# Two experts' scores in one visit of TensorE, new prices in a kernel's own list scheduler, and an order searched again

## The chip, the cores and the metric

The kernel runs on one core of a Trainium2 chip. Its engines work side by side: TensorE (PE in the profile, and PEld for its weight loads), VectorE (DVE), ScalarE (ACT), GpSimd (POOL) and SyncE (SP), which issues nearly all DMA transfers. The metric is the device time of one execution in microseconds; lower is better.

## The reference, cut to what matters

Four sequences of 576 tokens and width 512 pass through three stages. The second is the one whose code changes.

```python
# 1. windowed attention: 8 heads of 64; heads 0-3 see 32 keys back, heads 4-7 every 4th of 128 back
x = attn_out.transpose(0, 2, 1, 3).reshape(B, S, H * D)
# 2. mixture of E = 4 attention experts, the best K = 2 per token
for e in range(E):
    q, k, v = x @ wq[e], x @ wk[e], x @ wv[e]            # 64 wide
    scores = np.where(causal, -1e9, scale * (q @ k.transpose(0, 2, 1)))
    scores = scores - scores.max(-1, keepdims=True)
    a = np.exp(scores); a /= a.sum(-1, keepdims=True) + 1e-09
    ye = a @ v @ wo[e]                                   # added where e is among the best K, times its weight
# 3. layer norm, then x + relu(xn @ w_ch1) @ w_ch2, 512 -> 2048 -> 512
```

## The kernel before

All matrix products of fp32 data are made from pairs: a value rounded for TensorE ("h") and the rest ("l"), so a product is three matmuls (h·h, h·l, l·h). In the scores the two rests are packed: `KH` holds an expert's rounded keys on both halves of the partitions, `SQ` the rounded queries and their rests, `KL` the rests of the keys, so that two matmuls (`SQ`·`KH`, line 934, and `SQ`·`KL`, line 935) give a score tile. A third (line 937) adds the causal mask of the diagonal block: bf16, the identity as weights, `mdiag` as the moving tensor, 64 or 128 columns wide.

The kernel isn't ordered by hand. Each piece of work is a generator, a *chain*, that yields the steps it wants to do with an engine and a price in ns: `op("PE", ns, deps)`. `run_chains` holds a clock for each engine and for PSUM's eight banks (`places["bank"]`). It takes, again and again, the step that could start earliest by these clocks, ties broken by the rank of the chain, and writes its instructions then. What it writes down is the final order on each engine; on the chip the engines only wait for one another's results. So the prices have no effect on the chip except through the order, and through `either`, which lets the list choose between engines for a step (a copy out of PSUM by ACT or DVE, a scaling by DVE, POOL or ACT). `MODE` is what the list adds when TensorE goes from full 128-row matmuls (`None`) to matmuls on 64-column tiles (`"columns"`) or 64 x 64 tiles (`"quarters"`) and back. `SHIFT` and `LEANING` hold one number each for every chain: the first moves its rank, the second (ns) its bias against the first engine of an `either`. Both lists were found by search.

The chains that matter here: `scores`, `window` and `mix` are stage 1 (lines 629, 648 to 667, 679, 714 to 733). `value_tile` (line 756) and `project` (line 854) make values, keys and queries of the experts. `attend(b, pr_, i)` runs for 4 sequences, 2 pairs of experts and 5 query tiles; tile i sees n = 64, 192, 320, 448 or 576 keys. In it, for each of the two experts `ee`, in turn: one bank of PSUM (two for n = 576), the two score matmuls and the mask matmul, `put("s", ...)` after the second, the row maximum by DVE (line 947), the exponential with its row sum by ACT (line 949), after which the bank is free. Then both experts' sums are turned into weights (lines 953 to 957), the probabilities scaled (line 961 for the first 64 keys, line 967 by ACT or 969 by DVE or POOL for the others), transposed on TensorE (lines 977, 995, 1011) and multiplied by the values (lines 1026 to 1034). `out_proj` (line 1090) applies `wo`. `decode` (lines 1189 to 1217) turns the 64-bit weights of stage 3 into pairs; `mlp_group` (lines 1367 and 1394) is stage 3. Nothing separates the stages but the data: matmuls of stage 3 start at about 257 us, while `attend` still runs.

Of the kernel before, what the change touches and what calls it, by code (L numbers as in the profile page):

```python
# [39 lines left out]
]  # L40
LEANING = [
# [16 lines left out]
def windowed_attention_moe_mlp(  # L58
# [20 lines left out]
    P = 128  # L79
# [109 lines left out]
    for x in range(3):  # L189
# [18 lines left out]
    shared = {"DVE": 0.0, "POOL": 0.0}  # L208
    facts, chains, mode = {}, [], [None]
    shifts, leaning = list(SHIFT), list(LEANING)  # L210
    MODE = {(None, "columns"): 165.0, (None, "quarters"): 75.0, ("columns", None): 120.0, ("quarters", None): 100.0,
            ("columns", "quarters"): 65.0, ("quarters", "columns"): 65.0}

    def op(engine, ns, deps=(), tile=None):
# [1273 lines left out]
```

## Time and profile before

| what | value |
|---|---|
| median of 3 runs | 689.91 us (687.67 to 690.09) |
| the profiled execution | 688.62 us, of which the span from the first to the last instruction is 686.9 us |
| TensorE busy, weight loads busy | 672.9 us (98%), 568.8 us (83%) |
| VectorE, ScalarE, GpSimd busy | 497.7 us, 313.6 us, 197.6 us |
| granted clock of TensorE | 1.00 of full speed |

Busy time is the union of an engine's instructions. Matmuls overlap in the records (each lasts longer than the distance to the next one's start), so the cost of a matmul is read from start to start.

### The profile page before, as it was taken

To read this page: it belongs to the slowest core of one execution; us is meant where nothing else is said; L and a number is where in the kernel's file an instruction comes from. 1 tells how busy PE (TensorE), PEld (TensorE's weight loads), DVE (VectorE), ACT (ScalarE), POOL (GpSimd) and SP (SyncE) were. 2 spreads that over 40 slices of the span, in tenths; PEclk is the share of its full clock that TensorE was granted. 3 is DMA by queue.
4 is the path that set the end of the run, shared out by engine and by line. 5 is a ranking of instruction groups with operands and counts; after the bars stand their busy time and mean duration, and the time that the engine had idled before them with its cause. 6 is when DMAs were issued, how large, how long until landed. Compare 5 with 4: busy or idle time off the path is not lost.

```text
span 686.9 us, 13791 instructions
## 1 busy us (share of the span) xinstructions
PE 672.9 (98%) x5215; PEld 568.8 (83%) x5215; DVE 497.7 (72%) x1077; ACT 313.6 (46%) x879; POOL 197.6 (29%) x261
## 2 busy tenths in 40 slices
PE   7999999999999999999999999999999999999998
PEld 5788798988989887888888888888888888888886
DVE  6768999889888998988887755845755845754344
ACT  4767876888787889743322311211222211310110
POOL 3742112103211555565343321410422320410000
PEclk9999999999999999999999999999999999999999
DMA  9873643270403325335111200110111200100123
GB/s 175 206 154 94 107 89 69 53 125 12 103 16 128 108 82 180 106 103 176 43 62 62 62 31 31 62 31 1 62 62 32 62 31 2 60 1 0 62 92 123
DMA packets 111362, 52.55 MB, mean 77 GB/s; under 512 B 81472, under 2 KB 104512, under 8 KB 111296
## 3 DMA queue, kind: packets, MB, share of 16 engines
q1 hardware_dynamic: 110128, 51.38, 28.8%
q8 instruction: 41, 0.67, 0.4%
q10 hardware_dynamic: 1168, 0.29, 0.2%
q14 instruction: 25, 0.20, 0.1%
HBM read 39.86 MB, written 9.44 MB: 72 GB/s over the span
## 4 chain that ended last, share of the span: by engine, by line
PE 91%; DVE 4%; SPq 2%; ACT 1%; DMA 1%; issue 1%; POOL 0%; DVEq 0%; POOLq 0%
PE psall L1367 29%; PE psall L1394 29%; PE psall L854 7%; PE psall L756 4%; PE psall L1090 3%; PE psall L1034 2%; PE psall L714 2%; PE psall L679 2%; PE psall L934 2%; PE psall L1011 2%; PE psall L935 2%; PE psall L629 1%; PE psall L1032 1%; PE psall L565 1%; SPq L361 1%; DVE sm L663 1%
## 5 line engine op out<-in xcount | busy, mean ns | idle before, releaser
L1367 PE MATMUL psall<-xn,wp 128*128 128x512 f32 (+1 forms) x960 | 218.6, 372 | 0.0
L1394 PE MATMUL psall<-wp,ht 128*128 128x512 f32 (+1 forms) x870 | 217.0, 393 | 0.0
L1367 PEld LDWEIGHTS psall<-xn,wp 128*128 128x128 f32 x960 | 168.2, 188 | 34.7 <-issue 0.3
L1394 PEld LDWEIGHTS psall<-wp,ht 128*128 128x128 f32 x870 | 161.1, 188 | 36.5 <-issue 0.3
L1372 ACT ACTIVATE ht<-psall 128x512 fp32r<-128x512 f32 (+1 forms) x80 | 44.4, 554 | 221.0 <-PE psall L1367 211.3
L1403 DVE SCALAR_TENSOR_TENSOR x2a<-psall,rstd,x2a 128x512 f32<-128x512 f32 x124 | 91.7, 747 | 50.2 <-PE psall L1394 49.3
L1374 DVE SCALAR_TENSOR_TENSOR ht<-psall,ht 128x512 fp32r<-128x512 f32 (+1 forms) x80 | 50.8, 635 | 63.8 <-ACT ht L1372 63.5
L1205 POOL TENSOR_TENSOR d_pw<-d_pw,d_t 128x512 f32<-128x512 f32 x32 | 41.6, 1301 | 187.4 <-DVE d_pw L1202 184.8
L1217 POOL TENSOR_TENSOR wp<-d_pw,wp 128x512 fp32r<-128x512 f32 x32 | 42.5, 1328 | 28.8 <-ACT wp L1215 28.7
L949 ACT ACTIVATE Pp<-psall,nm 128x64 f32<-128x64 f32 (+4 forms) x80 | 42.3, 530 | 7.4 <-DVE nm L947 6.5
L947 DVE TENSOR_REDUCE nm<-psall 128x1 f32<-128x192 f32 (+4 forms) x80 | 38.1, 483 | 5.9 <-PE psall L937 4.7
L1215 ACT CAST wp<-d_pw 128x512 fp32r<-128x512 f32 x32 | 19.8, 620 | 48.9 <-DVE d_pw L1208 28.2
L667 POOL TENSOR_TENSOR sc<-sc,rs 128x480 f32<-128x480 f32 (+1 forms) x26 | 25.3, 975 | 52.1 <-DVE rs L665 47.6
L317 ACT COPY pT<-psall 80x288 f32<-80x288 f32 (+6 forms) x67 | 31.3, 476 | 12.3 <-PE psall L679 5.1
L1403 DVE SCALAR_TENSOR_TENSOR x2b<-psall,rstd,x2b 128x512 f32<-128x512 f32 (+1 forms) x33 | 24.2, 734 | 17.1 <-PE psall L1394 16.9
L1189 ACT ACTIVATE d_sq<-ws 128x512 f32<-128x512 f32 x32 | 21.5, 672 | 24.2 <-DVE d_pw L1208 18.0
L934 PE MATMUL psall<-KH,SQ 128*128 128x288 f32 (+4 forms) x96 | 31.8, 337 | 0.3 <-DVE xl L733 0.3
L1208 DVE SCALAR_TENSOR_TENSOR d_pw<-d_sq,d_pw 128x512 f32<-128x512 f32 x32 | 22.3, 696 | 11.0 <-POOL d_pw L1205 10.9
L679 PE MATMUL psall<-ident,sc 112*80 112x112 f32 (+1 forms) x168 | 25.2, 268 | 4.1 <-POOL sc L667 3.0
L935 PE MATMUL psall<-klz,SQ 128*128 128x288 f32 (+4 forms) x96 | 28.5, 302 | 0.0
L659 ACT ACTIVATE sc<-psall,mx 128x96 f32<-128x96 f32 (+1 forms) x113 | 27.4, 350 | 2.2 <-DVE mx L648 1.4
L1329 POOL TENSOR_TENSOR xn<-xt,xn 128x256 fp32r<-128x256 f32 (+1 forms) x24 | 22.8, 962 | 18.4 <-ACT xn L1325 15.4
(183 smaller groups left out, 1250.5 us busy)
## 6 DMA issues: line engine op xcount, KB each, us to landing
ws<-in_moe_w_ch_dram SPq DMA_DIRECT2D x32, 512.0 KB, 3.5
xd<-xg SPq DMA_DIRECT2D x18, 256.0 KB, 2.3
out_dram<-x2a SPq DMA_DIRECT2D x12, 256.0 KB, 2.0
xn<-xd SPq DMA_DIRECT2D x80, 32.0 KB, 1.8
KH<-KH SPq DMA_DIRECT2D x32, 72.0 KB, 2.0
natall<-in_q_dram SPq DMA_DIRECT2D x32, 72.0 KB, 2.6
natall<-in_k_dram SPq DMA_DIRECT2D x32, 72.0 KB, 2.3
xn<-xd SPq DMA_DIRECT2D x32, 64.0 KB, 2.8
```

The source lines that it names most:

```text
L679: nc.tensor.transpose(pt[:kw, P * (tt - a):P * (tt - a) + pw], sc[:pw, tt], ident[:pw, :pw])
L854: nc.tensor.matmul(pp[:, :HS], ws[:, c, pr_ * P:(pr_ + 1) * P], xs[:, c, cs], start=n == 0, stop=n == 3 * KC - 1)
L934: nc.tensor.matmul(ps[:m, :z - a], SQ[ee][:, q0:q0 + m], KH[ee][:, a:z], start=True, stop=False)
L935: nc.tensor.matmul(ps[:m, :z - a], SQ[ee][:, q0:q0 + m], KL[ee][:, a:z], start=False, stop=not end)
L949: nc.scalar.activation(pv, sv, AF.Exp, bias=nm[:m, ee:ee + 1], accum_out=sm[:m, ee:ee + 1])
L1205: nc.gpsimd.tensor_tensor(pf, pf, t1.bitcast(F32), op=ALU.add)
L1217: nc.gpsimd.tensor_tensor(lo, pf, hi.bitcast(F32), op=ALU.subtract)
L1367: nc.tensor.matmul(ph[:, :n_tok], ws[:, c * P:(c + 1) * P], xs[c], start=n == 0, stop=n == 3 * KC - 1)
L1372: nc.scalar.activation(hh[:, :n_tok], ph[:, :n_tok], AF.Relu)
L1374: nc.vector.scalar_tensor_tensor(hl[:, :n_tok], ph[:, :n_tok], 0.0, hh[:, :n_tok].bitcast(F32), op0=ALU.max, op1=ALU.subtract)
L1394: nc.tensor.matmul(po[:, :w], a_[:, sl], w_[:, cols], start=n == 0, stop=n == 3 * len(fs) - 1)
L1403: nc.vector.scalar_tensor_tensor(x2(i)[:, cols], po[:, :w], rstd[:, i:i + 1], x2(i)[:, cols], op0=ALU.mult, op1=ALU.add)
```

## The change

Five things change, all in the Python that writes the program.

1. In `attend`, tiles 0 to 3 do both experts' score matmuls in one step of TensorE. For i = 0 and 1 (n = 64 and 192) both experts share one bank, side by side; one mask matmul covers both diagonal blocks, one `tensor_reduce` gives both maxima. For i = 2 and 3 each expert has its bank; both banks are taken at once, the two mask matmuls follow one another, the two maxima stay apart. The exponentials stay two. Tile 4 keeps the old loop.
2. Prices in the list are set to others.
3. `MODE` gets other values, and SP steps get a `PATIENCE` of 27 ns in the comparison of start times (for the other engines it is 0 and changes nothing).
4. All of `SHIFT` and `LEANING` is replaced.
5. With 2 to 4 the order on every engine can differ everywhere, and so can the engine that an `either` picks.

```diff
 SHIFT = [
-    -2.04, -2.6, 4.96, -2.44, -0.7, 1.59, -0.29, 0.51, -0.3, -0.56, -2.11, 0.34, 0.68, -0.83, -0.79, -0.92, 1.36,
+    0.65, 0.67, 4.75, -1.44, -0.49, 1.13, 1.85, 1.2, -0.25, -0.36, 1, -0.24, 1.06, -0.58, -0.65, 0.61, 1.3, 0.94,
...
 LEANING = [
-    522, 471, 0, 71, 0, 0, 0, -105, 76, 0, 319, 0, 0, 0, 0, 0, 0, 0, 108, -52, 81, 243, 487, 28, 428, 453, 0, 0,
+    -226, -75, 0, 0, 0, 0, -113, 298, 43, 0, 319, 434, 0, 0, 128, 355, 343, 21, -348, 479, -384, 132, 736, 0, 632,
...
-    MODE = {(None, "columns"): 165.0, (None, "quarters"): 75.0, ("columns", None): 120.0, ("quarters", None): 100.0,
-            ("columns", "quarters"): 65.0, ("quarters", "columns"): 65.0}
+    PATIENCE = {"PE": 0.0, "ACT": 0.0, "DVE": 0.0, "POOL": 0.0, "SP": 27.0}
+    MODE = {(None, "columns"): 85.0, (None, "quarters"): 125.0, ("columns", None): 105.0, ("quarters", None): 105.0,
+            ("columns", "quarters"): 150.0, ("quarters", "columns"): 165.0}
...
-                    score = (at + change + sum(lean) + (0.0 if x or len(engines) == 1 else c[3]), c[0])
+                    score = (max(at + change, free[engine] + PATIENCE[engine]) + sum(lean) + (0.0 if x or len(engines) == 1 else c[3]), c[0])
...
-        t, e = yield either(("DVE*", dve(kw * nb)), ("POOL*", 1.98 * kw * nb), deps=[t])
+        t, e = yield either(("DVE*", dve(kw * nb)), ("POOL*", 2.08 * kw * nb + 20.0), deps=[t])
...
-            th = (yield op("ACT", act(n) + 20.0 + 0.85 * wide, [t, tx])) + 0.3 * wide
+            th = (yield op("ACT", act(n) + 30.0 + 0.95 * wide, [t, tx])) + 0.3 * wide
...
-        for ee in range(2):
+        if i < 4:
+            nb = 1 if i < 2 else 2
+            tb = yield acq("bank", nb)
+            pbs = [bank("s2") for _ in range(nb)]
+            pb = pbs[0]
+            w = n - q0
+            svs = [pb[:m, n * ee:n * ee + n] if nb == 1 else pbs[ee][:m, :n] for ee in range(2)]
+            t = yield op("PE", 4 * max(0.4415 * n + 5.0, 112.0) + 30.0 + 0.85 * w, [tb, tq])
+            for ee in range(2):
+                nc.tensor.matmul(svs[ee], SQ[ee][:, q0:q0 + m], KH[ee][:, :n], start=nb > 1 or not ee, stop=False)
+                nc.tensor.matmul(svs[ee], SQ[ee][:, q0:q0 + m], KL[ee][:, :n], start=False, stop=False)
+            if nb == 1:
+                both = pb[:m, :2 * n].rearrange("p (e n) -> p e n", e=2)
+                nc.tensor.matmul(both[:, :, q0:n], ident_bf, mdiag[:, None, :w].to_broadcast([P, 2, w]), start=False, stop=True)
+            else:
+                for ee in range(2):
+                    nc.tensor.matmul(svs[ee][:, q0:n], ident_bf, mdiag[:, :w], start=False, stop=True)
+            put("s", b, pr_, i, at=0.0)
+            tm = [t, t]
+            if nb == 1:
+                tm = [(yield op("DVE", dve(2 * n) + 20.0, [t]))] * 2
+                nc.vector.tensor_reduce(nm[:m], both, axis=AX.X, op=ALU.max, negate=True)
+            for ee in range(2):
+                Ps.append(Pp[:, ee])
+                if nb > 1:
+                    tm[ee] = yield op("DVE", dve(n) + 20.0, [t])
+                    nc.vector.tensor_reduce(nm[:m, ee:ee + 1], svs[ee], axis=AX.X, op=ALU.max, negate=True)
+                t1 = yield op("ACT", act(n) + 190.0, [tm[ee], tp])
+                nc.scalar.activation(Pp[:m, ee, :n], svs[ee], AF.Exp, bias=nm[:m, ee:ee + 1], accum_out=sm[:m, ee:ee + 1])
+                if nb > 1:
+                    give_bank(pbs[ee], t1)
+                tsum.append(t1)
+            if nb == 1:
+                give_bank(pb, t1)
+        for ee in range(2 if i > 3 else 0):
...
-                t = yield op("PE", 2 * max(0.4415 * (z - a) + 5.0, 90.0) + (100.0 if end else 0.0), [tb, tq])
+                t = yield op("PE", 2 * max(0.4415 * (z - a) + 5.0, 90.0) + (130.0 if end else 0.0), [tb, tq])
...
-                tpp[ee], e = yield either(("DVE*", 200.0 + 0.52 * (n - 64)), ("POOL*", 400.0 + 3.5 * (n - 64)), ("ACT", 135.0 + act(n - 64, False)), deps=[t])
+                tpp[ee], e = yield either(("DVE*", 200.0 + 0.52 * (n - 64)), ("POOL*", 330.0 + 2.8 * (n - 64)), ("ACT", 135.0 + act(n - 64, False)), deps=[t])
...
-        t = yield op("PE", 218.0 * (i + 1) if i else 125.0, tts + [tb], "columns" if i else None)
+        t = yield op("PE", 218.0 * (i + 1) + 30.0 if i else 125.0, tts + [tb], "columns" if i else None)
...
-        t = yield op("DVE", 340.0, [t, ta])
+        t = yield op("DVE", 440.0, [t, ta])
         nc.vector.tensor_scalar(t1, nh, 3, 0x3FFFFFF8, op0=ALU.logical_shift_left, op1=ALU.bitwise_and)
-        t = yield op("DVE*", 600.0, [t])
+        t = yield op("DVE*", 650.0, [t])
```

The other lines of the diff are of the last kind: prices of small DVE steps in the gate (80 to 160 ns before, 130 to 190 after), of the rest of `decode` (340 and 600 ns, now 440 and 650), of one scaling in `attend` (113, now 130), of the DVE step of `mix` and of a transpose in the layer norm.

## Rows read from the trace of the kernel before

**Rows 1.** The page: busy time of each engine, share of the span, instructions.

```profile
PE 672.9 (98%) x5215; PEld 568.8 (83%) x5215; DVE 497.7 (72%) x1077; ACT 313.6 (46%) x879; POOL 197.6 (29%) x261
```

**Rows 2.** The page: the chain that ended last, by engine.

```profile
PE 91%; DVE 4%; SPq 2%; ACT 1%; DMA 1%; issue 1%; POOL 0%; DVEq 0%; POOLq 0%
```

**Rows 3.** Busy by stretch: stretch, length, PE, PEld, DVE, ACT, POOL, clock, DMA.

```profile
100.00:130.00 30.00, 29.25 (x352) 26.04 (x351) 28.59 (x74) 22.32 (x74) 8.38 (x19) 1.00 0.28 62
...
160.00:190.00 30.00, 30.00 (x428) 27.49 (x426) 26.82 (x74) 25.27 (x81) 8.34 (x15) 1.00 0.29 66
...
250.00:281.00 31.00, 30.93 (x224) 24.93 (x223) 27.48 (x78) 28.70 (x85) 19.06 (x17) 1.00 0.46 141
```

**Rows 4.** The same view, before and after 281 us.

```profile
0.00:281.00 281.00, 270.20 (x3335) 238.46 (x3336) 239.61 (x663) 220.69 (x703) 93.55 (x170) 1.00 0.47 106
281.00:687.00 406.00, 402.66 (x1881) 330.38 (x1879) 258.11 (x414) 92.87 (x177) 104.02 (x92) 1.00 0.18 56
```

**Rows 5.** TensorE's waits from 15 to 281 us: total, times, longest; eight rows.

```profile
PE psall L679 <- POOL sc L667: 2.6, 5, 0.9
...
PE psall L679 <- DVE sc L667: 0.2, 1, 0.2
```

**Rows 6.** TensorE in order of time, visits among projections: start, length, instruction.

```profile
63.62 0.20 PE L934 MATMUL psall<-KH,SQ 128*128 128x64 f32 x1
63.65 0.27 PE L935 MATMUL psall<-klz,SQ 128*128 128x64 f32 x1
63.77 0.20 PE L937 MATMUL psall<-mdiag,ident_bf 128*128 128x64 bf16 x1
63.81 0.38 PE L854 MATMUL psall<-xh,wkh 128*128 128x288 f32 x1
64.02 0.29 PE L854 MATMUL psall<-xl,wkh 128*128 128x288 f32 x1
64.16 0.30 PE L854 MATMUL psall<-xh,wkl 128*128 128x288 f32 x1
...
64.79 0.23 PE L937 MATMUL psall<-mdiag,ident_bf 128*128 128x128 bf16 x1
64.83 0.38 PE L854 MATMUL psall<-xh,wqh 128*128 128x288 f32 x1
65.05 0.30 PE L854 MATMUL psall<-xl,wqh 128*128 128x288 f32 x1
```

**Rows 7.** All engines in order of time, a visit between transposes.

```profile
139.52 0.39 PE L934 MATMUL psall<-KH,SQ 128*128 128x320 f32 x1
...
139.75 0.31 PE L935 MATMUL psall<-klz,SQ 128*128 128x320 f32 x1
...
139.90 0.23 PE L937 MATMUL psall<-mdiag,ident_bf 128*128 128x128 bf16 x1
139.96 0.44 PE L1026 MATMUL psall<-pTh,V 128*128 128x128 f32 x2
```

**Rows 8.** DVE by line and form: busy, mean ns, idle before.

```profile
L947 DVE TENSOR_REDUCE nm<-psall 128x1 f32<-128x192 f32 x16 | 5.6, 351 | 1.3 <-PE psall L937 1.1
...
L947 DVE TENSOR_REDUCE nm<-psall 128x1 f32<-128x64 f32 x16 | 3.5, 218 | 0.6 <-PE psall L937 0.3
```

**Rows 9.** TensorE by line and form, the projections.

```profile
L854 PE MATMUL psall<-xh,wkh 128*128 128x288 f32 x64 | 21.8, 340 | 0.0
L854 PE MATMUL psall<-xh,wqh 128*128 128x288 f32 x64 | 21.0, 328 | 0.0
L854 PE MATMUL psall<-xl,wqh 128*128 128x288 f32 x64 | 18.8, 294 | 0.0
```

**Rows 10.** POOL by line and form, scalings that have a price in the list.

```profile
L667 POOL TENSOR_TENSOR sc<-sc,rs 128x480 f32<-128x480 f32 x20 | 20.3, 1016 | 47.5 <-DVE rs L665 44.8 <-ACT SQ L865 1.7 <-ACT sm L953 0.5
...
L969 POOL TENSOR_SCALAR Pp<-Pp,rs 128x256 f32<-128x256 f32 x3 | 2.9, 976 | 0.0
```

**Rows 11.** The widest scaling of `attend` on DVE, by line and form.

```profile
L969 DVE TENSOR_SCALAR Pp<-Pp,rs 128x512 f32<-128x512 f32 x7 | 3.3, 478 | 0.0
```

**Rows 12.** The same scaling on ACT, by line and form.

```profile
L967 ACT ACTIVATE Pp<-Pp,rs 128x512 f32<-128x512 f32 x8 | 5.7, 728 | 0.5 <-DVE rs L957 0.4
```

More of the change, by code (lines that the diff above doesn't have):

```diff
@@ L729, in mix @@
             wide = float(n) if dil else 0.0
-            th = (yield op("ACT", act(n) + 20.0 + 0.85 * wide, [t, tx])) + 0.3 * wide
+            th = (yield op("ACT", act(n) + 30.0 + 0.95 * wide, [t, tx])) + 0.3 * wide
             nc.scalar.copy(xv[0], pov)
-            tl = yield op("DVE", dve(n) + 20.0 + 0.72 * wide, [th])
+            tl = yield op("DVE", dve(n) + 30.0 + 0.85 * wide, [th])
             nc.vector.tensor_tensor(xv[1], pov, xv[0].bitcast(F32), op=ALU.subtract)
@@ L802, in gate @@
         row = [P, NT, E]
-        steps = [("DVE", 160.0, lambda n: n.tensor_tensor(gt, gj, ge, op=ALU.is_gt)),
-                 ("DVE", 160.0, lambda n: n.tensor_tensor(eq, gj, ge, op=ALU.is_equal)),
+        steps = [("DVE", 190.0, lambda n: n.tensor_tensor(gt, gj, ge, op=ALU.is_gt)),
+                 ("DVE", 190.0, lambda n: n.tensor_tensor(eq, gj, ge, op=ALU.is_equal)),
                  ("POOL", 340.0, lambda n: n.tensor_tensor(eq, eq, tri[:, None].to_broadcast(gb), op=ALU.mult)),
                  ("POOL", 340.0, lambda n: n.tensor_tensor(gt, gt, eq, op=ALU.add)),
-                 ("DVE", 160.0, lambda n: n.tensor_reduce(gw, gt, axis=AX.X, op=ALU.add)),
-                 ("DVE", 100.0, lambda n: n.tensor_reduce(gs, Gb, axis=AX.X, op=ALU.max)),
-                 ("DVE", 80.0, lambda n: n.tensor_scalar(gw, gw, 1.5, None, op0=ALU.is_lt)),
+                 ("DVE", 190.0, lambda n: n.tensor_reduce(gw, gt, axis=AX.X, op=ALU.add)),
+                 ("DVE", 150.0, lambda n: n.tensor_reduce(gs, Gb, axis=AX.X, op=ALU.max)),
+                 ("DVE", 130.0, lambda n: n.tensor_scalar(gw, gw, 1.5, None, op0=ALU.is_lt)),
                  ("POOL", 220.0, lambda n: n.tensor_tensor(ex, Gb, gs[:, :, None].to_broadcast(row), op=ALU.subtract)),
@@ L812, in gate @@
                  ("POOL", 220.0, lambda n: n.tensor_tensor(gw, gw, ex, op=ALU.mult)),
-                 ("DVE", 100.0, lambda n: n.tensor_reduce(gs, gw, axis=AX.X, op=ALU.add)),
+                 ("DVE", 150.0, lambda n: n.tensor_reduce(gs, gw, axis=AX.X, op=ALU.add)),
                  ("POOL", 220.0, lambda n: n.tensor_scalar(gs, gs, 1e-9, None, op0=ALU.add)),
-                 ("DVE", 100.0, lambda n: n.reciprocal(gs, gs)),
+                 ("DVE", 150.0, lambda n: n.reciprocal(gs, gs)),
                  ("POOL", 220.0, lambda n: n.tensor_tensor(gw, gw, gs[:, :, None].to_broadcast(row), op=ALU.mult))]
@@ L955, in attend @@
         nc.vector.reciprocal(rs[:m], sm[:m])
-        t = yield op("DVE*", 113.0, [t, tg])
+        t = yield op("DVE*", 130.0, [t, tg])
         nc.vector.tensor_tensor(rs[:m], rs[:m], gw[:m, i, 2 * pr_:2 * pr_ + 2], op=ALU.mult)
@@ L1197, in decode @@
         pw = wts.tile([P, DM], I32, tag="d_pw", name="d_pw", bufs=1)
-        t = yield op("DVE", 340.0, [t, ta])
+        t = yield op("DVE", 440.0, [t, ta])
         nc.vector.tensor_scalar(pw, t1, -0x800000, None, op0=ALU.bitwise_and)
         pf = pw.bitcast(F32)
-        t = yield op("DVE*", 600.0, [t])
+        t = yield op("DVE*", 650.0, [t])
         nc.vector.scalar_tensor_tensor(pf, nl.bitcast(U32), 2.0 ** -52, pf, op0=ALU.mult, op1=ALU.mult)
@@ L1206, in decode @@
         give("dt1", t)
-        t = yield op("DVE*", 600.0, [t, ts])
+        t = yield op("DVE*", 650.0, [t, ts])
         nc.vector.scalar_tensor_tensor(pf, sq, 2.0 ** -30, pf, op0=ALU.is_ge, op1=ALU.mult)
@@ L1318, in norm_tile @@
             for c2, l in enumerate(los):
-                t = yield op("DVE", 60.0 + 820.0 / len(los), [t, ta])
+                t = yield op("DVE", 20.0 + 790.0 / len(los), [t, ta])
                 nc.vector.transpose(xtv[:, :, w * c2:w * c2 + w],
```

54 rows, old and new, of tables (LEANING, SHIFT) are left out of this document.

## The prediction

> **What bounds the kernel now.** The page comes first: TensorE is busy for 672.9 of 686.9 us [rows 1], and the chain that ended last is TensorE for 91% [rows 2]. So look for TensorE's time, and ask what else could take its place. The table by stretch splits the span. After 281 us TensorE is busy for 402.66 of 406 us [rows 4]; it is never idle there but for the last 3.3 us, in which the last results are added and stored. That part is stage 3, whose matmuls the change doesn't touch. Before 281 us TensorE lacks 10.8 us [rows 4], half of them at the start. From 160 to 190 us it is busy for all 30.00 us; but from 100 to 130 us VectorE is at 28.59 of 30, nearly as full as TensorE, and from 250 to 281 us ScalarE is at 28.70 of 31 [rows 3]. The list of waits is short: from 15 to 281 us TensorE waits in eight ways, 2.6 us for the largest, 0.2 for the smallest [rows 5], 5.3 us together. So a microsecond taken from TensorE's work before 281 us should bring stage 3 forward by nearly as much, as long as VectorE and ScalarE, both close to full, follow.
>
> **The scores, one visit for two.** Busy time doesn't price a short matmul here; the distance between starts does. Take a visit between two projections. The mask starts at 63.77 and the next matmul at 63.81; that one's successor comes 0.21 later, where the pace of the same line is 0.14 (64.02 to 64.16). So a visit's mask costs 0.04 and then 0.07 or 0.08: about 0.12 us, though the mask has only 64 columns. With 128 columns it is the same: 0.04, then 0.22 [rows 6]. What is paid is the change of the kind of matmul, not the columns. A visit between transposes has another shape: 0.23 from its first to its second matmul, 0.15 from the second to the mask, both of 320 columns, so 0.08 on entry; then 0.06 from the mask to what follows [rows 7], 0.14 in all. The least that a mask takes is that 0.06 alone.
>
> Four sequences, two pairs and four tiles are 32 visits that end inside another one now. At 0.12 they are 3.8 us; the bounds are 32 x 0.06 = 1.9 and 32 x 0.14 = 4.5. Something stays: in 24 of them (tiles 1 to 3) the remaining mask work is wider by 128 columns or is a second matmul. 320 columns take 0.15 us [rows 7], so 128 take 0.06: up to 1.4 us, and nothing if it hides as the step from 64 to 128 columns did [rows 6]. I take the middle, 0.7. The term is **-3.1 us**, between -0.5 (1.9 less 1.4) and -4.5. The score matmuls themselves keep their number.
>
> The Trainium skill prices it otherwise. "TensorE: Matmul & The Clock Gate", section "Back-to-back issue gap", says that in a stream of weight loads and matmuls one of 128 columns takes about 81 ns, so the cost goes by the number of matmuls. Only 16 masks vanish (tiles 0 and 1); by that the term, as an estimate, is 1.3 us, and the two masks in a row of tiles 2 and 3 win nothing. The rows' 0.12 for a mask of either width speaks against it.
>
> **The maxima.** For tiles 0 and 1 one reduction replaces two, 16 fewer. One of 64 columns lasts 218 ns, one of 192 351 [rows 8], 1.04 ns a column; a joint one of 128 would last 285, so two of 218 lose 0.15 us. That is at most 2.4 us of VectorE, and nothing if their fixed parts overlap. On the end I count it as 0: VectorE is not on the chain but for 4% [rows 2]. It is cover for what follows, not a gain of its own.
>
> **Later first results.** In the old loop the first expert's maximum follows its own mask. Now it waits for the second expert's two matmuls, 0.12 each at 64 columns [rows 6]; for tiles 0 and 1 the joint reduction is longer by 0.07 or 0.20 us (64 or 192 columns at 1.04 ns), and ACT's first exponential waits for it. Behind that exponential on ACT stand copies out of PSUM, behind these TensorE's next transposes. I price it at 0: the list places other matmuls there, and it sees this delay in its own clocks. If that cover is gone, it is some 0.37 us for each of those 16 visits. For tiles 2 and 3 two banks of eight are taken at once; the second is held while the first expert's exponential runs. The same cover hides it.
>
> **Prices, patience, order.** None of these is work; each acts through the order. Two prices can be held against rows. The scaling of 480 columns on POOL was priced at 950 ns and is now at 1018; it lasts 1016. The one of 256 columns was at 1296, is now at 1047, and lasts 976 [rows 10]. Both move towards the chip, so the plan should describe it better, and the search started from that plan. What an order could win is bounded: the 5.3 us of waits, and the changes between transposes and projections. The same projection lasts 294 ns inside a stream but 340 and 328 on average where it is first of its three [rows 9]: 64 x 46 + 64 x 34 ns = 5.1 us. Together 10.4 us. What it could lose I bound by as much again. I take **-1.0 us**, a tenth of what is open: nearer prices speak for a gain, and these short waits leave little to find.
>
> **The sum** is made against the profiled execution: 688.62 - 3.1 - 1.0 = 684.5 us. That execution is 1.3 us below the median of the runs, and all four shown have a mean of 689.07; I add 0.45 for it and forecast **685.0 us**, 0.7% under 689.91.
>
> **The rivals.**
> A, the order wins much more: half of the 10.4 us, with the scores 3.1: 688.62 - 8.3 + 0.45 = 680.8. For it: the waits are spread over eight places, each short, as a better plan could clear. Against: from 160 to 190 us nothing is open but the changes of kind.
> B, the gain isn't to be had: VectorE, at 28.59 of 30 from 100 to 130 us [rows 3], sets the pace and TensorE's spare time turns into waits, or the merge is worth its lower bound of 0.5 us; with an order no better, 688.6 to 689.1. For it: the full VectorE. Against: TensorE at 30.00 of 30 elsewhere, where VectorE has three to five us to spare.
> C, one bank for two experts: in tiles 0 and 1 nothing leaves the bank until both experts are in it and one reduction is over. If the 0.37 us shows in each of 16 visits, it is 5.9: 685.0 + 5.9 = 690.9. For it: the waits that TensorE has are for results of just this kind, scaled probabilities that come late [rows 5]. Against: they are few. The Trainium skill, "Perfetto Trace Analysis", section "Matmuls", has the rule that would bring this: independent groups of matmuls should rotate through banks, so that one is emptied while the next is filled. No row of before shows two groups in one bank.
> D, slower: ScalarE becomes the bound from 250 to 281 us. The new prices make VectorE look dearer, in `decode` by 350 ns for each of 32 blocks, so `either` will send scalings and copies to ACT. A widest scaling frees 478 ns of VectorE [rows 11] and costs ACT 728 [rows 12]. ACT has 31 - 28.70 = 2.3 us left there, three of them; each further one pushes the end by up to 0.73. With 15 moved in all, 12 beyond the slack, the kernel is 8.7 us above the forecast, at the point where it is slower; with 17, 695.2. Against: the same scaling got cheaper on POOL too, which has 12 us to spare there [rows 3].
>
> **How the numbers follow.** A difference under 0.5%, 3.45 us, can't be told from no change here: faster is below 686.5, slower above 693.4. The forecast, from 682 to 687.5, has 0.47, of which 0.42 lies below 686.5. A has 0.13, all faster; B 0.20 and C 0.08, both the same; D 0.12, slower. That makes 0.55, 0.33 and 0.12. The range leaves out nearly all of D and the far end of A: 678.5 to 691.5.
>
> **What would show it.** Right: 16 fewer matmuls in TensorE's count; 64 reductions in the row maxima where there were 80; no second entry and exit inside a pair's visit, so that the starts of four score matmuls follow at 0.12 to 0.21 us and the mask costs 0.12 once; stage 3 as long as before, but starting some 4 us earlier; TensorE's waits before 281 us at or under 5.3 us. Wrong: a larger distance between the two score pairs or the two masks than I took; waits of TensorE for row maxima or exponentials (C); more scalings on ACT and ACT above 95% ahead of stage 3 (D); new waits for VectorE around 100 to 130 us (B). The weakest step is the order: nothing in the trace of before shows what a new one does, and a few waits of half a us each outweigh the scores.

## The result, and the profile after

The changed kernel takes 697.01 us (median of 6 runs, 694.86 to 698.26) where the kernel before takes 690.00 (687.67 to 690.98): a ratio of 1.0100, 95% interval 1.0082 to 1.0118. It is 1.0% slower; 685.0 was forecast, with a range up to 691.5. The profiled execution took 697.05 us, with a span of 695.3.

The page after, busy time and the chain by engine, against [rows 1] and [rows 2]:

```profile
PE 678.8 (98%) x5203; PEld 572.8 (82%) x5203; DVE 503.8 (72%) x1078; ACT 310.1 (45%) x865; POOL 197.4 (28%) x257
...
PE 87%; DVE 5%; ACT 3%; DMA 2%; issue 1%; POOL 1%; SPq 0%; DVEq 0%; POOLq 0%; ACTq 0%
```

There are 12 matmuls fewer: 16 masks are gone and 4 fillers more are there (useless matmuls that the list itself writes where its clock shows a hole on TensorE, 10 now and 6 before; so prices reach the chip in this way too, beside the order and the choice of an engine). And yet TensorE is busy for 5.9 us longer. Its idle time grew as well, from 14.0 to 16.5 us of the span. So both halves of its time got worse, and the chain shows nothing new that took TensorE's place. The windows tell where. First the halves of [rows 4], then the stretches of [rows 3]:

```profile
0.00:281.00 281.00, 267.72 (x3262) 236.02 (x3263) 237.12 (x640) 207.60 (x660) 92.12 (x165) 0.99 0.46 103
281.00:696.00 415.00, 411.12 (x1944) 336.73 (x1942) 266.70 (x439) 102.49 (x206) 105.30 (x93) 1.00 0.17 57
```

```profile
100.00:130.00 30.00, 29.59 (x468) 26.14 (x465) 28.36 (x76) 24.08 (x78) 7.72 (x14) 1.00 0.25 56
160.00:190.00 30.00, 29.25 (x379) 25.21 (x378) 28.24 (x80) 24.56 (x86) 6.11 (x13) 1.00 0.32 63
250.00:281.00 31.00, 30.35 (x223) 24.49 (x222) 26.59 (x73) 25.96 (x79) 15.11 (x15) 1.00 0.37 116
```

At 281 us TensorE has issued 73 matmuls fewer than before, and the remaining work takes 415 us where it took 406. The loss is made before 281 us. It has no single place: the stretch from 160 to 190 us, which was full, now lacks 0.75 us, and VectorE from 100 to 130 us and ScalarE from 250 to 281 us are less loaded than before, not more.

TensorE's waits from 15 to 281 us, against [rows 5]:

```profile
PE psall L680 <- POOL sc L668: 2.0, 4, 0.6
PE psall L1061 <- DVE klz L881: 1.0, 1, 1.0
PE psall L715 <- ACT pT L318: 0.8, 1, 0.8
PE psall L1125 <- DVE yl L1086: 0.7, 1, 0.7
...
PE psall L929 <- ACT pTh L318: 0.2, 1, 0.2
```

Twelve ways to wait instead of eight, 8.0 us instead of 5.3, and none of them is for a row maximum of the merged visit. The clock has a part too. Windows of two short stretches (the columns of [rows 3]) and TensorE's timeline with the waits ahead of them in brackets:

```profile
14.00:17.00 3.00, 2.97 (x18) 2.91 (x19) 2.46 (x6) 1.93 (x6) 1.39 (x3) 0.50 0.77 139
...
82.30:85.60 3.30, 3.30 (x14) 2.63 (x12) 2.15 (x6) 2.10 (x9) 0.00 (x0) 0.50 1.06 181
```

```profile
14.03 0.88 PE L680 MATMUL psall<-ident,sc 128*96 128x128 f32 x3 [1.15 <-POOL sc L668]
...
81.17 0.33 PE L1012 MATMUL psall<-ident,Ph 128*128 128x128 f32 x1 [0.30 <-DVE Ph L996]
82.14 1.29 PE L680 MATMUL psall<-ident,sc 112*80 112x112 f32 x6 [0.64 <-POOL sc L668]
83.11 0.72 PE L929 MATMUL psall<-KH,SQ 128*128 128x448 f32 x1
83.63 0.57 PE L930 MATMUL psall<-klz,SQ 128*128 128x448 f32 x1
84.00 0.57 PE L929 MATMUL psall<-KH,SQ 128*128 128x448 f32 x1
```

The granted clock is 0.50 there, the 1.2 GHz level, for 3.4 us each time, right behind waits. Score matmuls of 448 columns that follow one another start 0.37 us apart (83.63 to 84.00); at the 2.4 GHz level such starts are 0.20 apart in this trace. The profiled execution of before shows 1.0 in the same windows. The six runs of the changed kernel follow their mean clock: 694.86 us at 0.999, about 697 at 0.994 to 0.997, 698.26 at 0.993. So some 2 us of the 7 come and go with the clock, and 5 stay at full clock, for which one execution at 0.999 speaks.

**TensorE's time by kind.** From the start of each TensorE instruction to the start of the next, summed over the two traces by what the instruction is (worked out from the single records): transposes rise from 45.3 to 56.3 us, the matmuls on part of the array (64\*64, 64\*48, 128\*64, 80\*64, 96\*64) go from 72.2 to 71.9, scores and masks together from 37.5 to 36.4, all others from 526.2 to 525.0. Together that is the 8.4 us by which the span grew. The rise of the transposes is not their own time: there are 480 of them in both, a wait of the instruction behind a transpose is counted to the transpose here, and such waits make 6.1 of the 11.0 us; the stretches at half clock make 2.1.

With the usual pace of each kind and shape (its median) taken off, the growth has these parts: 3.4 us in distances that hold a recorded wait, 3.4 in the two stretches at half clock, and 1.7 in all the rest. In that rest one thing stands out. Changes between a transpose and a matmul on part of the array, without a wait, are 24 before, with 2.8 us above the usual pace, and 50 after, with 6.4. The other changes of kind fell from 401 to 298. One place in the timeline after shows two of them:

```profile
170.53 1.05 PE L630 MATMUL psall<-kT,qT 64*64 64x96 f32 x34
171.51 0.33 PE L1012 MATMUL psall<-ident,Ph 128*128 128x128 f32 x1
171.76 0.44 PE L1067 MATMUL psall<-pTh,V 128*64 128x128 f32 x4
172.03 0.39 PE L1069 MATMUL psall<-pT,V 128*64 128x128 f32 x4
```

A lone transpose stands between window scores and the experts' outputs. The last of the 34 starts at 171.34, 0.17 ahead of the transpose, where its like follow each other in 0.03 on average; from the transpose to the next start it is 0.25, where transposes of this shape in a row are 0.11 apart.

### The profile page after: what moved, and what is told of

The parts are those of the page before. It is cut to its first block, busy times and chain, and to the rows that moved or that the text cites. A ratio compares the mean times of both kernels' runs of the same rounds, so it can differ in the third digit from the quotient of the medians.

```text
span 695.3 us, 13740 instructions
## 1 busy us (share of the span) xinstructions
PE 678.8 (98%) x5203; PEld 572.8 (82%) x5203; DVE 503.8 (72%) x1078; ACT 310.1 (45%) x865; POOL 197.4 (28%) x257
## 4 chain that ended last, share of the span: by engine, by line
PE 87%; DVE 5%; ACT 3%; DMA 2%; issue 1%; POOL 1%; SPq 0%; DVEq 0%; POOLq 0%; ACTq 0%
PE psall L1429 29%; PE psall L1402 28%; PE psall L855 6%; PE psall L757 4%; PE psall L1125 3%; PE psall L715 3%; PE psall L680 2%; PE psall L1069 2%; PE psall L1046 2%; PE psall L630 1%; PE psall L930 1%; PE psall L929 1%; PE psall L1067 1%; PE psall L566 1%; PE psall L1030 1%
## 5 line engine op out<-in xcount | busy, mean ns | idle before, releaser
L1438 DVE SCALAR_TENSOR_TENSOR x2b<-psall,rstd,x2b 128x512 f32<-128x512 f32 (+1 forms) x33 | 24.2, 734 | 13.9 <-PE psall L1429 13.3
L318 ACT COPY pT<-psall 128x512 f32<-128x512 f32 (+6 forms) x59 | 27.7, 477 | 13.2 <-PE psall L680 6.0
L948 ACT ACTIVATE Pp<-psall,nm 128x320 f32<-128x320 f32 (+3 forms) x64 | 30.4, 479 | 3.1 <-DVE nm L946 1.1
L660 ACT ACTIVATE sc<-psall,mx 128x80 f32<-128x80 f32 (+1 forms) x120 | 29.2, 348 | 5.4 <-DVE mx L649 3.2
L1364 POOL TENSOR_TENSOR xn<-xt,xn 128x256 fp32r<-128x256 f32 (+1 forms) x20 | 20.2, 1020 | 32.6 <-ACT xn L1360 32.6
L318 DVE COPY pT<-psall 80x288 f32<-80x288 f32 (+6 forms) x45 | 23.4, 528 | 2.9 <-PE psall L680 2.1
L757 PE MATMUL psall<-wvh,xh 128*128 128x260 f32 x80 | 24.4, 304 | 0.0
L1230 DVE SCALAR_TENSOR_TENSOR d_t<-ws,d_t 128x512 int32<-128x512 int32 x32 | 23.2, 724 | 0.6
```

What stands on the lines that cost most here:

```text
L318: (nc.scalar.copy if engine == "ACT" else nc.vector.tensor_copy)(dst, src)
L757: nc.tensor.matmul(pv[:, :NV], xs[:, c, q0:q0 + P], ws[:, c], start=c == 0 and n == 0, stop=c == KC - 1 and n == 2)
L948: nc.scalar.activation(Pp[:m, ee, :n], svs[ee], AF.Exp, bias=nm[:m, ee:ee + 1], accum_out=sm[:m, ee:ee + 1])
L1438: nc.vector.scalar_tensor_tensor(x2(i)[:, cols], po[:, :w], rstd[:, i:i + 1], x2(i)[:, cols], op0=ALU.mult, op1=ALU.add)
```

## The experiments

Two theories were on the table. Theory 1: the merged visit is harmless and the order that came with the new prices loses the time. Theory 2: the merged visit itself costs, by later results or its one bank. As the runs came in, theory 1 split further, and each expectation numbers its own two. All ratios are to runs of the kernel before on the same chip, which had medians from 689.94 to 690.19; a ratio is not the quotient of the two medians.

| run | us | ratio, 95% |
|---|---|---|
| masks apart again | 696.70 | 1.0086 (1.0062 to 1.0110) |
| fillers in waits | 695.94 | 1.0070 (1.0049 to 1.0092) |
| before without masks of tiles 0 to 3 | 685.54 | 0.9920 (0.9898 to 0.9943) |
| before, tiles 0 and 1 merged | 690.97 | 1.0007 (0.9988 to 1.0026) |
| before, order searched on | 691.38 | 1.0022 (1.0002 to 1.0041) |
| changed, order searched on | 695.42 | 1.0075 (1.0043 to 1.0108) |
| changed, short work on POOL | 694.69 | 1.0064 (1.0043 to 1.0085) |
| before, short work on POOL | 689.15 | 0.9977 (0.9958 to 0.9996) |
| merge with old prices | 692.85 | 1.0017 (0.9995 to 1.0038) |
| the same, another search | 694.48 | 1.0057 (1.0036 to 1.0078) |
| new prices, no merge | 701.00 | 1.0142 (1.0110 to 1.0173) |
| new list's steps only | 697.84 | 1.0106 (1.0079 to 1.0134) |
| new durations only | 694.42 | 1.0056 (1.0040 to 1.0072) |
| changed, another search | 703.91 | 1.0202 (1.0164 to 1.0240) |

**Masks apart again.** The order of the changed kernel, each expert with its own mask:

```diff
                 nc.tensor.matmul(svs[ee], SQ[ee][:, q0:q0 + m], KL[ee][:, :n], start=False, stop=False)
-            if nb == 1:
...
-                    nc.tensor.matmul(svs[ee][:, q0:n], ident_bf, mdiag[:, :w], start=False, stop=True)
+                nc.tensor.matmul(svs[ee][:, q0:n], ident_bf, mdiag[:, :w], start=False, stop=nb > 1 or ee == 1)
```

> The changed kernel with its order of all instructions kept; only each expert's score matmuls get their own mask matmul again, behind their own pair, in 32 visits. Theory 1 (the merge is a gain, the new order loses more than it gives): slower than the changed kernel by 32 x 0.12 us less the wider or second mask that goes (0 to 1.4), so 2.4 to 3.8 us, 699.4 to 700.8. Theory 2 (the merge itself hurts, by results that come later): the matmuls of a visit are still adjacent, so no more than the masks' own time comes back; 697 to 698 if the masks are hidden anyway, which would take the forecast's 0.12 away.

It took 696.70, below both ranges and no longer than the changed kernel, so the loss isn't in the masks, and the gain that was forecast for them isn't there either. The same visit in the timelines, first the changed kernel, then this one:

```profile
145.47 0.19 PE L929 MATMUL psall<-KH,SQ 128*128 128x64 f32 x1
145.49 0.28 PE L930 MATMUL psall<-klz,SQ 128*128 128x64 f32 x1
145.60 0.28 PE L929 MATMUL psall<-KH,SQ 128*128 128x64 f32 x1
145.72 0.28 PE L930 MATMUL psall<-klz,SQ 128*128 128x64 f32 x1
145.83 0.23 PE L933 MATMUL psall<-mdiag,ident_bf 128*128 128x128 bf16 x1
145.87 0.37 PE L757 MATMUL psall<-wvh,xh 128*128 128x260 f32 x1
```

```profile
145.41 0.19 PE L929 MATMUL psall<-KH,SQ 128*128 128x64 f32 x1
145.44 0.28 PE L930 MATMUL psall<-klz,SQ 128*128 128x64 f32 x1
145.55 0.20 PE L931 MATMUL psall<-mdiag,ident_bf 128*128 128x64 bf16 x1
145.59 0.28 PE L929 MATMUL psall<-KH,SQ 128*128 128x64 f32 x1
145.71 0.28 PE L930 MATMUL psall<-klz,SQ 128*128 128x64 f32 x1
145.82 0.21 PE L931 MATMUL psall<-mdiag,ident_bf 128*128 128x64 bf16 x1
145.87 0.36 PE L757 MATMUL psall<-wvh,xh 128*128 128x260 f32 x1
```

0.40 us from the first score to the next work instead of 0.46. The mask in the middle cost its 0.04 and no second change of kind. Where no wait stands in them, the visits are on average some 0.05 us shorter when merged (0.03 at 64 columns, 0.06 in the wider tiles): about 1.7 us for 32. The two visits of a pair stay side by side in this run, so that is the worth of the masks alone. The executions of this kernel had a granted clock of 0.998 to 1.0 and those of the changed one 0.993 to 0.999, so the two medians can't show it; the three at 1.0 took 695.74 to 696.66 us, the one of the changed kernel at 0.999 took 694.86.

**The price of a mask.** The order of before, frozen, with the masks of tiles 0 to 3 left out:

```diff
-                nc.tensor.matmul(ps[:m, :z - a], SQ[ee][:, q0:q0 + m], KL[ee][:, a:z], start=False, stop=not end)
-                if end:
+                nc.tensor.matmul(ps[:m, :z - a], SQ[ee][:, q0:q0 + m], KL[ee][:, a:z], start=False, stop=not end or i < 4)
+                if end and i > 3:
```

> The kernel before with its order kept, without the 64 mask matmuls of tiles 0 to 3: the causal mask of these tiles is left out. It prices a mask. Forecast's price of 0.12 us each: 7.7 us faster, 682.3. Rival, 81 ns for a matmul and its weight load: 5.2 us, 684.8. Rival B of the forecast (VectorE sets the pace, TensorE's time is worth little): under 3 us, 687 or above.

64 masks are worth 690.19 - 685.54 = 4.65 us, 0.073 each. By the interval of the ratio it is 3.9 to 7.0, which shuts out the 7.7 of the forecast's price and the "under 3" of rival B. The timeline of this kernel at the visit of [rows 6]:

```profile
64.28 0.19 PE L934 MATMUL psall<-KH,SQ 128*128 128x64 f32 x1
64.31 0.27 PE L935 MATMUL psall<-klz,SQ 128*128 128x64 f32 x1
64.42 0.38 PE L854 MATMUL psall<-xh,wkh 128*128 128x288 f32 x1
64.63 0.29 PE L854 MATMUL psall<-xl,wkh 128*128 128x288 f32 x1
64.76 0.29 PE L854 MATMUL psall<-xh,wkl 128*128 128x288 f32 x1
```

No mask is there, and still the first projection takes 0.21 to its successor, then 0.13. Here the slow first step that the forecast put on the mask's bill stays without the mask. It isn't so behind wider scores. One visit of 320 columns, before and then without its mask:

```profile
199.54 0.30 PE L935 MATMUL psall<-klz,SQ 128*128 128x320 f32 x1
199.68 0.23 PE L937 MATMUL psall<-mdiag,ident_bf 128*128 128x128 bf16 x1
199.72 0.38 PE L854 MATMUL psall<-xh,wkh 128*128 128x288 f32 x1
199.94 0.30 PE L854 MATMUL psall<-xl,wkh 128*128 128x288 f32 x1
```

```profile
198.26 0.30 PE L935 MATMUL psall<-klz,SQ 128*128 128x320 f32 x1
198.40 0.29 PE L854 MATMUL psall<-xh,wkh 128*128 128x288 f32 x1
198.54 0.30 PE L854 MATMUL psall<-xl,wkh 128*128 128x288 f32 x1
```

From the second score to the second projection it is 0.40 us with the mask and 0.28 without. Set side by side in this way, the two traces price a mask at its place. Ahead of projections and values it is 0.04 us behind scores of 64 columns, 0.10 behind 192 and 0.13 behind 320 and 448; ahead of transposes it is 0.07 to 0.08 behind 192. Over 61 of the 64 places, those without a recorded wait, it adds up to 4.8 us, so nearly all that TensorE saves reaches the end.

**Merging in the old order.** Tiles 0 and 1 merged at the first expert's place, in the order of before (one bank, one mask, one reduction, both exponentials in a row):

```diff
+                if i < 2:
...
+                    if not ee:
+                        nc.tensor.matmul(both[:, :, q0:n], ident_bf,
+                                         mdiag[:, None, :n - q0].to_broadcast([P, 2, n - q0]), start=False, stop=True)
...
+            elif not ee:
+                nc.vector.tensor_reduce(nm[:m], both, axis=AX.X, op=ALU.max, negate=True)
```

> The kernel before with its order kept; in tiles 0 and 1 the first expert's step of TensorE does both experts' score matmuls into one bank with one mask, VectorE takes both maxima in one reduction and ScalarE both exponentials in a row at the first expert's places; the second expert's places stay empty. Theory 1: 16 masks fewer at 0.12 us and nothing lost, 1.0 to 1.9 us faster, 688 to 689. Theory 2 (one bank for two experts hurts, rival C): up to 4 us slower, 690 to 694.

690.97 and 1.0007: on balance nothing is lost or won, which misses theory 1 and lies in theory 2's range. TensorE's waits rise by some 0.85 us in its trace, among them two of 0.3 for exponentials. The 16 masks alone are worth about 1 us (0.04 and 0.08 each, from the run without masks), so the merged visit costs about as much as it gives: as an estimate from the two runs 1.5 us, 0.1 for each of the 16 visits, and with the interval of the ratio anything from 0.2 to 2.8. That is far from the 0.37 each of rival C, and not shown to be nothing.

**Waits.** Two runs with the order of the changed kernel price them. One puts useless matmuls into five of its waits ahead of 85 us, the other lets POOL scale one column of each block of window probabilities:

```diff
+    FILL = {11: 1, 12: 5, 134: 3, 136: 1, 137: 3}
...
+                    for _ in range(FILL[picked[0]]):
+                        nc.tensor.matmul(b, ident_bf, ident_bf[:, None].to_broadcast([P, 4, P]), start=True, stop=True)
```

```diff
+        z = kw if e == "DVE" else 1
-            sc, sc, rs[:, :, None].to_broadcast([P, nb, kw]), op=ALU.mult)
+            sc[:, :, :z], sc[:, :, :z], rs[:, :, None].to_broadcast([P, nb, z]), op=ALU.mult)
```

> The changed kernel with its order kept; 13 matmuls of no use (bf16, 512 columns, into a bank that is free) stand in front of five steps for which TensorE waited in the changed kernel's trace: one and five ahead of the two waits at 12.4 and 14.0 us, seven ahead of the three from 80 to 82 us. They fill 3.0 us of waits, and cost up to 0.2 us each where they overshoot. Theory 1a (the two stretches at half clock, 3.4 us each from 14.0 and 82.2 us, are part of the loss): the clock stays at 1.00 and the kernel is 2 to 3 us faster than the changed one, 694 to 695. Theory 1b (the clock's fall lies inside time that is waited away anyway): same within 1 us or slower by the overshoot.

> Order of the changed kernel, frozen; the scalings of the window's probabilities that fall to POOL do one column of each block only, so the rest of these probabilities goes unscaled. TensorE's waits for POOL (3.1 us in the changed kernel's profile, the largest group) should be gone. Theory 1 (these waits, and the half clock that follows some of them, make a good part of the 7 us) expects 692.5 to 694. Theory 2 (spread thin over changes of kind and many waits; what POOL gives is lost at the next wait) expects 695 to 696.5.

> The same with the order of the kernel before: POOL's scalings do one column of each block. Its waits for POOL are 2.6 us. Theory 1 expects 687 to 688, theory 2 689 to 690; the difference from the run with the changed order is what POOL's lateness adds in that order.

The fillers gave 1.1 us and left the clock at 0.998 to 1.0: some of the clock's share, not the rest; 694 to 695 was not reached. Short work on POOL gave 2.3 us in the changed order (694.69, between the ranges of its two theories) and 0.8 in the old one (theory 2's range), so POOL's lateness explains some 1.5 us of the difference, 0.9 by the ratios. The waits of the changed order without POOL's work:

```profile
PE psall L630 <- DVE kT L318: 1.2, 2, 0.7
PE psall L1062 <- DVE klz L882: 1.1, 1, 1.1
PE psall L716 <- ACT KH L869: 0.8, 1, 0.8
...
PE psall L681 <- POOL sc L669: 0.6, 1, 0.6
```

3.1 us of waits for POOL became 0.6, and the next ones remain.

**Merge and prices parted.** From here only the two lists, the prices and the visits differ. A search changed single entries of SHIFT and LEANING and kept what made the list's own end earlier; the plan is what the list lays out by its clocks. First, orders near the two kernels:

> Kernel before with its prices and its visits; only the two lists are searched on from where they stand, so the order is another one that its plan rates as long as the old one. Theory 1 (an order's time on the chip is a matter of luck within several us: orders that a plan rates equal differ by its errors) expects a difference of 2 to 5 us to either side. Theory 2 (with the old prices the plan describes the chip about equally well for any order searched from it; the loss of the new kernel comes with its prices) expects 689 to 691, within 1 us of before.

> Changed kernel, all as it is; only the two lists are searched on, to an order that its plan rates slightly shorter. Theory 1 (luck of the order) expects 691 to 699, most likely nearer to 694 than the 697 of the changed kernel. Theory 2 (the new prices lead every order astray) expects 695 to 697.5.

1.4 us above before, between the ranges of its two theories, and 1.6 below the changed kernel, inside both: these neighbours of an order are worth a microsecond or two, not seven. Next, the merge without the prices and the prices without the merge:

```diff
-    MODE = {(None, "columns"): 85.0, (None, "quarters"): 125.0, ("columns", None): 105.0, ("quarters", None): 105.0,
-            ("columns", "quarters"): 150.0, ("quarters", "columns"): 165.0}
+    MODE = {(None, "columns"): 165.0, (None, "quarters"): 75.0, ("columns", None): 120.0, ("quarters", None): 100.0,
+            ("columns", "quarters"): 65.0, ("quarters", "columns"): 65.0}
```

That is the changed kernel with the old list's steps; the old durations go with them in the first two runs. The third has the new ones, and the old loop over the experts.

> The merged visits of the changed kernel with all of the old prices and without the patience; lists searched on from the old ones (scaled until they build) to an order that the plan rates as long as that of the kernel before. Theory 1 (the prices led the search astray, the merge itself is harmless and its masks are worth about 1 us): 688 to 690, not slower than before. Theory 2 (the merged visit itself costs, by its later first results and its one bank, in any order): 693 to 697, as the changed kernel.

> The same merge and old prices, another search that got stuck at an order which the plan rates about 4 us longer than the one of the run beside it. If the plan's length carries over to the chip, 692 to 694; if an order's length on the chip is luck, anything from 688 to 698 whatever the plan says.

> The kernel before with its visits apart, the new prices and the patience, lists searched on; the plan rates this order 4 us longer than the one of the changed kernel. Theory 1 (the new prices lead astray): 696 to 702, slower than before with no merge at all, and above its own plan by more than orders from the old prices are. Rival (the new prices describe the chip better, and only the search stopped early): at most 694.

The merge with old prices took 692.85, between the ranges of its two theories. The interval of its ratio (1.0017) holds 1, and its median is 2.7 us above before. Its executions had a granted clock of 0.992 to 0.998; the three at 0.998 took 689.78 to 692.05. So it isn't shown to be as fast as before, but the merge by itself, in this order, lacks most of the 7 us: theory 2 of the merge, 693 to 697, is not borne out. The second search took 694.48, just above the 692 to 694 of its plan's length: four executions at a clock of 1.0 took 692.2 to 693.3, four at 0.990 took 695.9 to 696.7. The prices without the merge lose 1.4%; 701.00 is in theory 1's range, and the rival's "at most 694" falls. In the trace of the first, changes between transposes and matmuls on part of the array, counted as above, are 33, against 24 before and 50 in the changed kernel. Its halves, to be read beside [rows 4]:

```profile
0.00:281.00 281.00, 267.43 (x3297) 0.99 0.47 105
281.00:691.00 410.00, 406.08 (x1898) 1.00 0.18 56
```

Its loss to before is of the kinds known by now: 13.57 us without TensorE ahead of 281 us instead of 10.80, and a stretch at half clock.

**Which prices, or the search?**

> The kernel before with its visits apart and its old durations; only the list's steps are new, the prices of a change of kind on TensorE and the patience. Lists searched on; the plan rates the order 8 us longer than that of the kernel before. Theory 1 (the new prices of changes make the list avoid direct changes, and bring transposes between: the order's loss comes from them): 696 to 700, with the waits and the dear changes of the changed kernel. Theory 2 (any set of prices gives orders several us apart, according to where the search ends, and the chip follows the plan's length): also 697 to 700, but then the run with the new durations alone is as much above its own plan, and so is the other search of the changed kernel.

> The kernel before with its visits apart and the old list's steps; only the new durations of instructions on VectorE, ScalarE, POOL and TensorE. The plan rates this order 6 us longer than that of the kernel before. Theory 1 (the list's steps are at fault): 689 to 692, near before. Theory 2 (the chip follows the plan's length, whatever the prices): 695 to 698.

> The changed kernel with all its prices and its merged visits, lists from another start and another search, which ended at an order that the plan rates 4 us longer than the one in the changed kernel. Theory 1 (the prices are worse than the old ones as a description, so the plan's length says little): 695 to 698, as the changed kernel. Theory 2 (the chip follows the plan's length; where a search ends decides): 699 to 702.

The list's steps alone lose 7.8 us and the durations alone 4.4; neither half of the prices is innocent. The third run has the program and the prices of the changed kernel, and lists from another search: 703.91, 6.9 us slower still. TensorE ahead of 281 us in it:

```profile
0.00:281.00 281.00, 263.89 (x3206) 0.98 0.46 102
```

17.1 us without TensorE there instead of 13.3. The first of the three lies in the ranges of both its theories, the second between them, the third above both. Theory 1 of the first, that the new steps bring transposes between the groups, is not borne out: counted as above, the changes between transposes and matmuls on part of the array are 42 with the steps alone, 37 with the durations alone, 42 with all new prices and no merge, and 48 in the second merge with old prices. They follow neither the steps nor the time.

**The plan's length.** The expectations set the ends of plans against one another across different prices, and so mix the order with the level of the prices. The order of before ends at 677.9 us by its own prices. Laid out again with other prices (worked out from the kernels' lists alone, without the chip), the same order ends at 678.5 by the new steps, 683.3 by the new durations and 683.6 by all of them; so of the "6 us longer" of the durations alone, 5.4 are the prices. Against the order of before at the same prices, in us:

| prices | order | plan | chip |
|---|---|---|---|
| old | before, order searched on | -0.2 | +1.4 |
| old | merge with old prices | -0.6 | +2.7 |
| old | the same, another search | +3.2 | +4.4 |
| new steps | new list's steps only | +7.0 | +7.8 |
| new durations | new durations only | +0.6 | +4.4 |
| all new | the changed kernel | -1.5 | +7.0 |
| all new | changed, order searched on | -2.1 | +5.5 |
| all new | changed, another search | +2.5 | +13.9 |
| all new | new prices, no merge | +2.8 | +10.9 |

With the steps alone the search ended at an order that its own plan rates worse, and the chip followed the plan. With all new prices the plan rates the changed kernel 1.5 us better than the order of before, and the chip has it 7.0 worse. By the old prices the chip is 1.2 to 3.3 us above the plan in this comparison, by all new ones 7.5 to 11.4. Where the visits are merged, the plan contains what its prices give for that; and these are single orders, so the sizes are rough. No order here beat the kernel before.

## Why the prediction was wrong

**What bounds the kernel** was read rightly: time lost or saved by TensorE ahead of 281 us came out at the end (without the masks 4.8 us saved there, 4.65 at the end), and stage 3 took as long as before (it lacks TensorE for 3.9 us of 415, where it was 3.3 of 406).

**The scores, -3.1 us: mis-sized.** The failing step is "So a visit's mask costs 0.04 and then 0.07 or 0.08". The 0.04 is right; at the very place of [rows 6], behind scores of 64 columns, the 0.07 is paid with or without the mask, as the run without masks shows. Behind scores of 320 and 448 columns the 0.12 is right after all. Measured, a mask is worth 0.073 us on average over tiles 0 to 3, and the masks of the 32 merged visits 1.7 us, inside the bounds of 0.5 to 4.5 but not near the value taken. What it gives to join the visits themselves was not measured alone. The rule that was set against it, "Back-to-back issue gap" on the page "TensorE: Matmul & The Clock Gate" of the Trainium skill, has about 81 ns for a matmul of 128 columns; as an estimate by it 64 masks are 5.2 us. 4.65 were measured: on average the rule was nearer than the forecast's reading of one row, though place by place the masks run from 0.04 to 0.13.

**The maxima, 0.** The joint reduction came out as the forecast's line gave it. DVE by line and form:

```profile
L941 DVE TENSOR_REDUCE nm<-psall 128x2 f32<-128x128 f32 x8 | 2.3, 285 | 1.2 <-PE psall L933 1.2
```

285 ns, as forecast, against 218 for one of 64 columns [rows 8]; no wait of TensorE for it appears.

**Later first results, 0: small, but not shown to be nothing.** The order of before with merged visits of tiles 0 and 1 is level with before, so they take back about the 1 us that its 16 masks give. Rival C's 5.9 us falls. The Trainium skill's advice to rotate banks ("Perfetto Trace Analysis", section "Matmuls") has no more than that estimated 0.1 us a visit behind it here; the largest new wait for an exponential was 0.3.

**Prices, patience, order, -1.0: this failed**, by some 8 to 10 us, and with its sign: with 1.7 us for the masks, the 7.0 us by which the kernel is slower leave 8.7 for this term and the one above together. The step was "nearer prices speak for a gain, and these short waits leave little to find". Two prices of POOL did move towards the chip, though POOL's scaling of 480 columns lasts 989 ns in the trace after, as near to the old 950 as to the new 1018. The set as a whole did not describe the chip better where it mattered: by it the changed kernel is 1.5 us ahead of the order of before, and on the chip 7.0 behind. Where a search ends counts too: searches from the same program and prices ended at 697.0 and 703.9 us, at 692.9 and 694.5 with the old ones. The forecast took the order of the kernel before for something that any new search would reach; no new search here reached it. What the new order costs in the profiled execution is 3.4 us of longer waits, 3.4 at half clock and 1.7 of all the rest; the forecast had no term for the clock. The bound on the loss, "by as much again" as 10.4 us, held the 8; the value taken from it had no row behind it. The second part of that step, the changes of kind, was also looked at in the wrong place: the projections of [rows 9] changed little (328 and 340 ns before, now the two below; by the forecast's own sum 4.4 us instead of 5.1),

```profile
L855 PE MATMUL psall<-xh,wqh 128*128 128x288 f32 x64 | 21.5, 335 | 0.0
L855 PE MATMUL psall<-xh,wkh 128*128 128x288 f32 x64 | 20.6, 321 | 0.1
```

while the changes between transposes and matmuls on part of the array grew by 3.6 us.

**The rivals.** A didn't come. B came nearer than the forecast in the merge's worth (0.5 us, where the masks gave 1.7), not in the time and not in its cause: VectorE is less full from 100 to 130 us, and without the masks nearly all of TensorE's saved time reached the end. D named the right side by the wrong mechanism: ScalarE fell from 28.70 to 25.96 us of 31, and its scalings of 512 columns rose from 8 to 9, not by 15. The rival that was missing is the plain one: the new order is worse, by many short waits, by the half clock behind some of them and by changes of kind. The prediction's last sentence names it, as its weakest step, and gave it no chance of its own.

**What stays open.** That the loss is in the main the new order's and not the merge's is shown. Why the new prices rate such orders well is not: no run parts the single durations. All six orders from new prices ended later (both halves alone, all without the merge, and three with it), but their starts differed, and the old prices, too, gave one as late as 694.5. That waits bring the half clock is read from their order in time in several traces; no run took the clock alone away.

## What to carry to other kernels

Where an edit makes a planner lay the work anew, price the order as a draw with its own spread, here 1.4 to 14 us, all to the slow side of a well searched order, and set the edit's small gains against that. Before trusting new prices, lay the old order out with them and hold its end against the new one's: here they called an order better that lost 7 us. Test an edit first in the old order, frozen: there the merge could be priced within 0.2%. And take the price of a short matmul from the same place with and without it, at more than one place: the slow step behind it belonged to its neighbour in one and to the mask in another.

## What the runs showed of the hardware

A transpose alone between two groups of matmuls on part of the array (four in the changed kernel, one of them at 171.51 above) costs about 0.10 us ahead of it and 0.15 behind it above the usual pace, without a wait in the trace. Score matmuls of 64 columns start 0.11 us apart in a row, though the first of them among projections is followed after 0.03 (145.47 above); the next full-width projection then takes 0.21 instead of 0.13. Behind scores of 320 columns it takes 0.14 (198.40), and 0.22 once a bf16 mask stands between (199.72). And TensorE fell to its 1.2 GHz level for 3.4 us at a time behind waits of only 0.6 to 1.2 us (13.97 and 82.24 us in the changed kernel), which the kernel before mostly escapes: on the chip where it ran 28 times, 23 executions had a granted clock of 0.998 or more.
